# Two experts change places in a routed attention and expert kernel, with SyncE's order of loads and the output buffers

## The chip, the cores and the metric

The kernel runs on one core of a Trainium2 chip. A core has five engines that work side by side: TensorE (matrix products, with a queue of its own for loading weights), VectorE, ScalarE, GpSimd and SyncE, which here issues most of the transfers. The metric is the device time of one execution in microseconds (us).

## The reference

The inputs are q, k, v of 2 batches x 8 heads x 768 tokens x 64, 16 cluster centroids per head, and the weights of the two later stages. What is computed, cut to its core:

```python
# stage 1: attention within clusters
mask   = argmax(q_n @ c_n) == argmax(k_n @ c_n)          # per head
scores = where(mask, q @ k.T / 8, -1e9)
x      = softmax(scores) @ v                             # (2, 768, 512)
# stage 2: one of 8 experts per token
logits, local_gate = x @ w_gate, sigmoid(x @ w_local)
e      = argmax(logits[s]) if s == 0 or local_gate < 0.5 else e_of_the_token_before
x[s]   = softmax(logits[s])[e] * (relu(x[s] @ w1[e]) @ w2[e])   # w1 512x1024, w2 1024x512
# stage 3: gated projection
gate   = sigmoid(causal convolution of x with conv_w, 5 taps)
out    = (gate * (x @ w_val)) @ w_out                    # (2, 768, 512)
```

All of it is wanted in float32. w_val and w_out are given as 64-bit floats and are converted on the chip.

## The kernel before, in words

**Stage 1** runs over 8 groups of two heads. While its last groups run, the routing of tokens is worked out in four quarters of 384 tokens. A quarter's rows (512 values, the softmax weight and the token's number) are scattered by GpSimd into `xslots`, a table in DRAM with a range of rows for each expert, and are also copied whole to `xall` (`keep_rows`), which only the overflow loop reads. Experts 0, 1 and 2 have two ranges, one for each batch.

**Stage 2** takes the experts in 8 places, k = 0 to 7. Places 0, 1, 6 and 7 have fixed experts (the table `AT`, from place to expert); places 2 to 5 take experts 4 to 7 in the order of their token counts, which the chip works out. `CAPS` gives the number of rows (tokens) that a place computes; for the experts with two ranges `ROWS` gives the rows of batch 0 and of batch 1. Tokens beyond these would be done by a loop behind an `If` after the last place. Before the change the widths are 128, 176, 300, 240, 224, 176, 192, 192.

The expert of place 0 is begun early: its batch 0 rows, 128 of them, are loaded, transposed and multiplied during the end of stage 1 (`early_load`, `early_rows`, `early_products`). Place 0 itself then does batch 1. For each place `load_x` reads the rows, `do_x` transposes them on TensorE and casts them to `xhi`, for places 2 to 4 also to a low part `xlo`; `do_mm1` makes the first product (the weights are loaded 128 x 128, the rows stream past as columns), relu on ScalarE and the low part of the result on VectorE; `do_mm2` the second product, in which the rows are loaded as weights and 512 columns of w2 stream past, and `mm2_out` scales and scatters the result to `x2d` in DRAM. Where a tile has 64 rows (`FOLD`, `PACK`) its high and low parts lie side by side in one load of weights, so that it takes 16 matmuls instead of 24; ScalarE and VectorE then add the two halves of the result. Places 6 and 7 do their second product by batch with `do_half`: both places' batch 0 first, then the reload of batch 0 from `x2d`, then both places' batch 1.

**Weights.** An expert has four pieces of 1 MB, (k,0) and (k,1) for the first product, (k,2) and (k,3) for the second. Some are used whole; the others are loaded into one of three staging buffers (`stg`, by `w_stage`), cast by ScalarE (L360, two halves) and reduced to a low part by VectorE (L366, two halves). A staging buffer is free for the next piece when the second subtraction is done. The ring of finished pieces has four places.

**The order.** Nothing is scheduled by a planner: each engine's instructions stand in program order, and SyncE issues its transfers in order too, so that one which waits holds up all behind it. Small steps are spread over the products by `tick`, which is called after each quarter of a first product and after each tile and half of a second one. A tick takes one step from `work` (the casts and subtractions of a piece, the second of them with the load of the next piece), two from `late` (the overflow bookkeeping, on VectorE) and one, sometimes two, from `conv`, the conversion of w_val and w_out. The conversion has 66 steps: 8 chunks, each a load (L260), four VectorE steps (L230 to L238), one of ScalarE (L265, L266), two of GpSimd (L269 and L270, L273) and a store (L276, L277). Its buffer `wspace` is the memory in which the token rows stood before (so its first load waits for `keep_rows(3)`) and into which the rows of stage 3 are reloaded (L1330). What is left of it after batch 0's `do_half` is issued there (L1324).

**Stage 3** transposes the reloaded rows (L1377), makes the value product (L1421, L1422, L1427), the convolution and the gate, and the output product; `project_out` copies a tile of 128 rows from PSUM into a buffer `os` and stores it.

Of the kernel before, what the change touches and what calls it, by code (L numbers as in the profile page):

```python
# [8 lines left out]
F32 = mybir.dt.float32  # L9
# [10 lines left out]
NQT = 6  # L20
NC_ = 16
E = 8
CAPS = (128, 176, 300, 240, 224, 176, 192, 192)
WHOLE = (0, 1, 5, 6, 7)
PACK = 64
AT = {0: 0, 1: 3, E - 2: 2, E - 1: 1}
HALVED = (0, 1, 2)
ROWS = {0: (128, 128), 1: (96, 96), 2: (128, 64)}
V = E + len(HALVED)
NF = len(AT)  # L30
NS = E - NF
SLOT = 428
# [9 lines left out]
def routed_attention_moe_kernel(  # L42
# [289 lines left out]
    def w_stage(at):  # L332
        if pending:
            j = pending.pop(0)
            home[j] = at
            wraw[j] = at.tile([128, 2048], F32, tag="w", name="wraw")
            w_load(j, wraw[j])
# [456 lines left out]

    def early_load():
        EA["xs"] = xin_p.tile([128, 2, S], F32, tag="x", name="exs")[:, 0, :XC]
        nc.sync.dma_start(EA["xs"], xslots[0:128, :])

    def early_rows():
        xs = EA["xs"]  # L800
# [245 lines left out]
    def tick():  # L1046
# [13 lines left out]
    XT, HT, IDS, PW = {}, {}, {}, {}  # L1060
    NT = [-(-c // 128) for c in CAPS]
    FOLD = [
        ROWS[AT[k]][1] == PACK if k and AT.get(k) in HALVED else 0 < (c - 1) % 128 < PACK and n > 1
        for k, (c, n) in enumerate(zip(CAPS, NT))
    ]
    TR = [
# [1 line left out]
    ]  # L1068
    XS = {}

    def load_x(k):
        if k >= E:
            return
        n, rows = NT[k], TR[k]
        XS[k] = xs_p.tile([128, -(-WX[k % 2] // 128), XC], F32, tag=f"xs{k % 2}", name="xs")
        if k == 0:
            nc.sync.dma_start(XS[k][:, 0, :], xslots[E * SLOT:E * SLOT + 128, :])
            return
        if AT.get(k) in HALVED:
            for t, c in enumerate((AT[k], E + HALVED.index(AT[k]))):  # L1080
                nc.sync.dma_start(XS[k][:TR[k][t], t, :], xslots[c * SLOT:c * SLOT + TR[k][t], :])
            return
        if k in AT:
            src = xslots[AT[k] * SLOT:AT[k] * SLOT + CAPS[k], :]
        else:
            src = xslots[bass.ds(turn[k] * SLOT, CAPS[k]), :]
        if FOLD[k] or k == 0:
            for t, r in enumerate(rows):
                nc.sync.dma_start(XS[k][:r, t, :], src[sum(rows[:t]):sum(rows[:t]) + r, :])
        else:  # L1090
            nc.sync.dma_start(XS[k][:rows[0], :n, :], src.rearrange("(t p) c -> p t c", p=rows[0]))
# [140 lines left out]
        for t in sorted(range(n), key=lambda t: (not FOLD[k] or t < n - 1, t)):  # L1232
            mm2_out(k, t)

    def do_half(k, t, *apart):
        YP[k, t] = ps_y.tile([128, 512], F32, tag="y", name="yp")
        for q in range(2):
            mm2_part(k, t, q, *mm2_weights(k, q))
            tick()
        mm2_out(k, t, *apart)  # L1240
# [5 lines left out]
    for n, k in enumerate(free):  # L1246
        turn[k] = nc.sync.value_load(ordi[0:1, n:n + 1], min_val=NF, max_val=E - 1)
    w_stage(stg[2])
    queue_split(R + 2)
    ey = ps_y.tile([128, 512], F32, tag="y", name="ey")  # L1250
    for q in range(2):
# [6 lines left out]
    y = y_p.tile([128, 512], F32, tag="y", name="ysb")  # L1258
    nc.scalar.activation(y, ey, AF.Copy, scale=EA["pw"])
    scatter(x2d, EA["ids"], y, 2 * S, "rows of different tokens")  # L1260
    work += [lambda: None, lambda: None, lambda: keep_rows(3)]
    late += overflow_steps()
    do_mm1(0)
    XS["ready"] = True
    do_mm2(0)
    do_mm1(1)
    for k in range(2, E - 1):
        do_mm1(k)
# [200 lines left out]
    def project_out(b, t, parts=1):  # L1469
        op = OP.pop((b, t))  # L1470
        r0 = S * b + 128 * t
        os_ = fl.tile([128, 512], F32, tag="os", name="os")
        w = 512 // parts
        for n in range(parts):
            cs_ = slice(w * n, w * n + w)
            (nc.vector.tensor_copy if n else nc.scalar.copy)(os_[:, cs_], op[:, cs_])
            (nc.scalar if n else nc.sync).dma_start(out[r0:r0 + 128, cs_], os_[:, cs_])
# [108 lines left out]
```

## Time and profile before

| | |
|---|---|
| median of three runs | 541.88 us (541.17 to 542.16) |
| the profiled execution | 539.74 us, of which its span is 538.1 us |
| TensorE busy | 515.7 us, 96% of the span |
| VectorE, ScalarE, GpSimd busy | 353.1, 310.0, 91.3 us |
| mean granted TensorE clock | 0.99 of full speed |
| moved by all transfers | 108.63 MB, 202 GB/s over the span |

The span reaches from the first to the last instruction; all times in the rows are microseconds from its start. A busy share says how long an engine had an instruction running, not that the time hung on it: for that one looks at the waits. Names such as `wraw<-in_wq_dram` stand for a result and what it is made from, L360 for line 360.

### The profile page before, as it was taken

Reading aid. Unit: us, or ns where it says so; the run is one execution under the profiler, and the core shown is the slowest. Engines: PE = TensorE matmul, PEld = TensorE weight load, DVE = VectorE, ACT = ScalarE, POOL = GpSimd, SP = SyncE. Lnnn points to the kernel's source line nnn. Section 1 sums busy time; section 2 is a strip of 40 time slices with the busy share of each in tenths; the row PEclk is TensorE's granted clock in tenths of the full one; section 3 lists DMA queues with packets and bytes.
Section 4 is the critical chain, followed back from the end, with each engine's and each line's share of the span. In section 5 each row is a group of like instructions: output and inputs, shape, how many; then the busy total and the mean of one; then the engine's idle time right before and its main releaser. Section 6 shows DMA issues by size and latency. Waiting matters only on the chain.

```text
span 538.1 us, 8817 instructions
## 1 busy us (share of the span) xinstructions
PE 515.7 (96%) x3189; PEld 409.4 (76%) x3190; DVE 353.1 (66%) x693; ACT 310.0 (58%) x592; POOL 91.3 (17%) x106
## 2 busy tenths in 40 slices
PE   7898999999999999999999499999999999999996
PEld 3775777777677767776956498979889887899885
DVE  5684767575677877655603679986367673599960
ACT  3696868677776778675112355645334463485632
POOL 5011002020203031000310020523421344100000
PEclk9899999999999999999999889999999999999999
DMA  5876787888887866810665866795978855730023
GB/s 146 225 157 212 154 278 198 242 231 207 267 202 272 191 214 135 294 47 2 201 250 193 314 213 222 242 325 194 362 242 314 311 177 203 266 139 2 19 99 117
DMA packets 35524, 108.63 MB, mean 202 GB/s; under 512 B 4718, under 2 KB 5230, under 8 KB 30869
## 3 DMA queue, kind: packets, MB, share of 16 engines
q1 hardware_dynamic: 32341, 101.15, 60.7%
q0 software_dynamic: 2176, 6.31, 3.2%
q10 hardware_dynamic: 960, 0.58, 0.4%
q8 instruction: 26, 0.43, 0.3%
q14 instruction: 21, 0.17, 0.1%
HBM read 58.39 MB, written 29.83 MB: 164 GB/s over the span
## 4 chain that ended last, share of the span: by engine, by line
PE 41%; DMA 5%; SPq 1%; DVE 1%; ACT 1%; issue 1%; ACTq 0%; DVEq 0%
PE hps L1155 13%; PE yp L1195 4%; PE yp L1197 4%; PE yp L1196 4%; PE vp L1421 2%; PE vp L1427 2%; PE vp L1422 2%; PE op L1467 2%; PE op L1466 2%; PE op L1465 2%; DMA xall<-xnat 2%; PE yp L1192 1%; PE yp L1193 1%; DMA wraw<-in_wq_dram 1%; PE xp L1118 1%
## 5 line engine op out<-in xcount | busy, mean ns | idle before, releaser
L675 DVE TENSOR_REDUCE mx<-s 128x1 f32<-128x768 f32 x96 | 91.6, 954 | 59.5 <-PE s L668 53.4
L704 ACT COPY pt<-tp 128x384 f32<-128x384 f32 x148 | 65.7, 483 | 54.4 <-PE tp L699 54.3
L684 ACT ACTIVATE pexp<-s,mx 128x768 f32<-128x768 f32 x96 | 87.1, 907 | 6.7 <-DVE mx L675 4.5
L699 PE MATMUL tp<-ident,pexp 128*128 128x128 f32 x576 | 81.1, 277 | 0.3 <-DVE pt L702 0.2
L699 PEld LDWEIGHTS tp<-ident,pexp 128*128 128x128 f32 x576 | 68.2, 142 | 7.7 <-ACT pt L704 3.3
L366 DVE TENSOR_TENSOR wlo<-wraw,whi 128x1024 fp32r<-128x1024 f32 x40 | 52.9, 1330 | 29.6 <-ACT whi L360 29.6
L711 PE MATMUL pv<-pt,vt 128*64 128x384 f32 x360 | 67.8, 498 | 0.0
L360 ACT CAST whi<-wraw 128x1024 fp32r<-128x1024 f32 x40 | 40.7, 1046 | 31.8 <-DMA wraw<-in_wq_dram 16.8
L664 PE MATMUL s<-st 128*128 128x384 f32 x188 | 57.3, 386 | 1.5 <-ACT pexp L684 1.5
L1155 PE MATMUL hps<-xhi,wone 128*128 128x192 f32 (+2 forms) x320 | 50.7, 318 | 0.0
L668 PE MATMUL s<-st 80*128 80x384 f32 x188 | 49.0, 342 | 1.4 <-DMA st<-ohr 1.4
L1155 PEld LDWEIGHTS hps<-xhi,wone 128*128 128x128 f32 x320 | 49.0, 195 | 1.6 <-ACT xhi L1124 0.6
L664 PEld LDWEIGHTS s<-st 128*128 128x128 f32 x188 | 28.6, 191 | 17.8 <-issue 7.3
L711 PEld LDWEIGHTS pv<-pt,vt 128*64 128x64 f32 x360 | 21.9, 136 | 23.8 <-issue 23.8
L1162 ACT ACTIVATE h<-hps 128x352 fp32r<-128x352 f32 (+5 forms) x36 | 16.9, 474 | 33.8 <-PE hps L1155 33.7
L1195 PE MATMUL yp<-whi,h 128*112 128x512 f32 (+4 forms) x88 | 35.0, 397 | 0.8 <-ACT h L1162 0.8
L668 PEld LDWEIGHTS s<-st 80*128 80x128 f32 x188 | 34.4, 190 | 1.7 <-issue 1.7
L1197 PE MATMUL yp<-whi,h 128*112 128x512 f32 (+4 forms) x88 | 34.7, 394 | 0.0
L1196 PE MATMUL yp<-wlo,h 128*112 128x512 f32 (+4 forms) x88 | 34.7, 394 | 0.0
L384 POOL TENSOR_TENSOR xx<-xkq,xx 128x768 fp32r<-128x768 f32 x8 | 14.6, 1822 | 117.5 <-ACT xx L378 117.5
L1407 DVE SCALAR_TENSOR_TENSOR gt<-xf,convw_sb,gt 128x768 f32<-128x768 f32 x32 | 32.0, 1015 | 0.4
L1165 DVE SCALAR_TENSOR_TENSOR h<-hps,h 128x128 fp32r<-128x128 f32 (+7 forms) x52 | 18.4, 391 | 16.7 <-ACT h L1162 15.1
(280 smaller groups left out, 893.0 us busy)
## 6 DMA issues: line engine op xcount, KB each, us to landing
wraw<-in_wq_dram SPq DMA_DIRECT2D x20, 1024.0 KB
st<-xx SPq DMA_DIRECT2D x48, 384.0 KB
wone<-in_wq_dram SPq DMA_DIRECT2D x12, 1024.0 KB
xslots<-padrow SPq DMA_DIRECT2D x15, 771.0 KB
xkq<-in_kq_dram SPq DMA_DIRECT2D x15, 384.0 KB
wspace<-in_wd_dram SPq DMA_DIRECT2D x8, 512.0 KB
xall<-xnat SPq DMA_DIRECT2D x4, 771.0 KB
vt<-in_v_dram SPq DMA_DIRECT2D x8, 384.0 KB
```

What stands on the lines that cost most here:

```text
L366: nc.vector.tensor_tensor(lo[:, c], t[:, c], hi[:, c].bitcast(F32), op=ALU.subtract)
L664: nc.tensor.matmul(ps[:, n, :384], st[:, 1, q0:q0 + 128], st[:, 0, 384 * n:384 * n + 384], start=True, stop=False)
L668: nc.tensor.matmul(ps[:, n, :384], st[0:80, 2, q0:q0 + 128], st[0:80, 3, 384 * n:384 * n + 384], start=False, stop=True)
L675: nc.vector.tensor_reduce(mx, ps[:, :, :384], axis=AX.XY, op=ALU.max, negate=True)
L684: nc.scalar.activation(pt, ps[:, :, :384], AF.Exp, bias=mx[:, 0:1], accum_out=Zt[i // 6][:, t, h:h + 1])
L699: nc.tensor.transpose(tp[:, k, :], p[:, 128 * kt:128 * kt + 128], ident)
L704: nc.scalar.copy(dst, tp)
L711: nc.tensor.matmul(PVs[u][64 * h:64 * h + 64, :], Vt[g][:, kt, h, :], PT[u, h][:, kt, :], start=(kt == 0), stop=(kt == NQT - 1), skip_grou ...
L1155: nc.tensor.matmul(hp, a[:, d, fs], c[:, d, :w], start=(n + d == 0), stop=(n + d == len(terms) + 2))
L1195: nc.tensor.matmul(yp[:r], h[:, fa, hi], whv[:, f, :], start=(q == 0 and f == 0), stop=False)
L1196: nc.tensor.matmul(yp[:r], h[:, fa, hi], wlv[:, f, :], start=False, stop=False)
L1197: nc.tensor.matmul(yp[:r], h[:, fa, lo], whv[:, f, :], start=False, stop=(q == 1 and f == 3))
```

## The change

The change has four parts. Place 0 gets expert 1 and place 7 expert 0; the early tile is now expert 1's batch 0, with 128 rows as before, and place 0 computes 72 rows instead of 128. Place 7 has 64 rows of batch 0, which are folded, and 96 of batch 1, with the folded tile put second (`halves`, and the exchange in `do_half`); place 6 has 120 and 64 rows instead of 128 and 64. `keep_rows(3)` is issued by SyncE right behind the load of piece (2,0) instead of by the first tick of place 0's second product; two empty steps stand ahead of the first piece's casts instead of behind them; and the conversion begins after place 0's second product instead of before it. The output tiles have four buffers instead of two.

```diff
-CAPS = (128, 176, 300, 240, 224, 176, 192, 192)
+CAPS = (72, 176, 300, 240, 224, 176, 184, 160)
 WHOLE = (0, 1, 5, 6, 7)
 PACK = 64
-AT = {0: 0, 1: 3, E - 2: 2, E - 1: 1}
+AT = {0: 1, 1: 3, E - 2: 2, E - 1: 0}
 HALVED = (0, 1, 2)
-ROWS = {0: (128, 128), 1: (96, 96), 2: (128, 64)}
+ROWS = {1: (128, 72), 2: (120, 64), 0: (64, 96)}
...
     def early_load():
         EA["xs"] = xin_p.tile([128, 2, S], F32, tag="x", name="exs")[:, 0, :XC]
-        nc.sync.dma_start(EA["xs"], xslots[0:128, :])
+        nc.sync.dma_start(EA["xs"], xslots[AT[0] * SLOT:AT[0] * SLOT + 128, :])
...
     FOLD = [
-        ROWS[AT[k]][1] == PACK if k and AT.get(k) in HALVED else 0 < (c - 1) % 128 < PACK and n > 1
+        PACK in ROWS[AT[k]] if k and AT.get(k) in HALVED else 0 < (c - 1) % 128 < PACK and n > 1
...
+    def halves(k):
+        cols = AT[k], E + HALVED.index(AT[k])
+        return cols[::-1] if ROWS[AT[k]][0] == PACK else cols
+
     def load_x(k):
...
         if k == 0:
-            nc.sync.dma_start(XS[k][:, 0, :], xslots[E * SLOT:E * SLOT + 128, :])
+            c = E + HALVED.index(AT[0])
+            nc.sync.dma_start(XS[k][:CAPS[0], 0, :], xslots[c * SLOT:c * SLOT + CAPS[0], :])
             return
         if AT.get(k) in HALVED:
-            for t, c in enumerate((AT[k], E + HALVED.index(AT[k]))):
+            for t, c in enumerate(halves(k)):
...
-    def do_half(k, t, *apart):
+    def do_half(k, b, *apart):
+        t = b ^ (ROWS[AT[k]][0] == PACK)
         YP[k, t] = ps_y.tile([128, 512], F32, tag="y", name="yp")
...
     w_stage(stg[2])
+    keep_rows(3)
+    work += [lambda: None, lambda: None]
     queue_split(R + 2)
...
-    work += [lambda: None, lambda: None, lambda: keep_rows(3)]
     late += overflow_steps()
     do_mm1(0)
+    do_mm2(0)
     XS["ready"] = True
-    do_mm2(0)
     do_mm1(1)
...
-        os_ = fl.tile([128, 512], F32, tag="os", name="os")
+        os_ = fl.tile([128, 512], F32, tag="os", name="os", bufs=4)
```

## Rows read from the trace of the kernel before

**Rows 1.** The chain of waits, 286 to 309 us: start, duration, what.

```profile
286.72 1.05 ACT whi L360
287.80 1.23 DVE wlo L366
...
292.68 8.17 DMA xall<-xnat
301.00 3.46 DMA wspace<-in_wd_dram
...
305.04 0.69 DVE wspace L231
...
307.80 0.70 DVE xlo L1129
```

**Rows 2.** Timeline of TensorE, 293 to 315 us: start, duration, instruction, [idle before, releaser].

```profile
293.36 4.94 PE L1155 MATMUL hps<-xhi,wone 128*128 128x176 f32 x32
...
308.54 1.45 PE L1118 MATMUL xp<-ident,xs 128*128 128x128 f32 x6 [6.85 <-DVE xlo L1129]
309.92 4.24 PE L1155 MATMUL hps<-xhi,wone 128*128 128x176 f32 x16
313.87 0.83 PE L1155 MATMUL hps<-xhi,whi 128*128 128x300 f32 x4
```

**Rows 3.** Windows: length, busy time by engine (PE first), PEclk, DMA share, GB/s.

```profile
302.00:309.00 7.00, 0.46 (x2) 0.46 (x3) 4.39 (x18) 1.24 (x2) 0.00 (x0) 0.81 0.99 390
```

**Rows 4.** Timeline of TensorE, 440 to 463 us.

```profile
440.08 0.47 PE L1195 MATMUL yp<-whi,h 128*128 128x512 f32 x1 [0.81 <-ACT h L1162]
...
451.30 0.39 PE L1192 MATMUL yp<-whi,h 128*128 128x512 f32 x1
...
460.55 1.47 PE L1377 MATMUL x2p<-ident,x2nat 128*128 128x128 f32 x12
462.98 0.44 PE L1421 MATMUL vp<-xh,whi 128*128 128x384 f32 x1 [0.95 <-ACT xh L1381]
```

**Rows 5.** Timeline of the end of the kernel.

```profile
532.86 0.39 PE L1467 MATMUL op<-whi,gl 128*128 128x512 f32 x1
533.37 1.06 ACT L1476 COPY os<-op 128x512 f32<-128x512 f32 x2 [1.46 <-DMA out_dram<-os]
```

**Rows 6.** Timeline of SyncE's issues: first start, from there to the last one's end.

```profile
279.24 11.41 SPq L326 DMA_DIRECT2D wraw<-in_wq_dram  x2
```

**Rows 7.** Timeline of ScalarE, the first cast of piece (2,1).

```profile
295.71 1.05 ACT L360 CAST whi<-wraw 128x1024 fp32r<-128x1024 f32 x1 [5.81 <-DMA wraw<-in_wq_dram]
```

**Rows 8.** The chain of waits, first products of places 3, 4 and 7.

```profile
337.60 5.39 PE hps L1155 x48
...
364.01 5.36 PE hps L1155 x48
...
428.87 10.41 PE hps L1155 x64
```

**Rows 9.** Timeline of ScalarE in place 7, the conversion's pair and the relu behind it.

```profile
433.77 0.63 ACT L265 ACTIVATE wspace<-wspace 128x512 f32<-128x512 int32 x1
...
434.82 0.49 ACT L1162 ACTIVATE h<-hps 128x384 fp32r<-128x384 f32 x1
```

**Rows 10.** Timeline of GpSimd, 448 to 458 us.

```profile
448.98 1.29 POOL L269 TENSOR_TENSOR wspace<-wspace 128x512 f32<-128x512 f32 x1 [1.06 <-ACT wspace L265]
...
453.04 0.95 POOL L635 DMA_INDIRECT x2d<-ysb,ids  x1 [0.16 <-issue]
...
457.59 0.92 POOL L635 DMA_INDIRECT x2d<-ysb,ids  x1 [3.61 <-DVE ysb L1207]
```

**Rows 11.** SyncE's waits, 450 to 470 us: total, times, longest.

```profile
SPq L1330 <- DMA whd<-wspace: 1.3, 1, 1.3
SPq L1330 <- DMA wld<-wspace: 0.8, 1, 0.8
```

**Rows 12.** Timeline of SyncE, the reload.

```profile
456.04 9.41 SPq L1330 DMA_DIRECT2D x2nat<-x2d  x5
```

## The prediction

> **What bounds the kernel now.** I read the table of busy shares first: TensorE is busy for all but a few per cent of the span, so a gain is either TensorE work that goes away or one of its few waits. The chain of waits, in order of time, shows where those are. The first is at 292 to 309 us: the copy of the last token rows takes 8.17 us, the load of the conversion's first chunk can only start behind it and takes 3.46 us, VectorE stands at the two steps that need this chunk, and place 2's low parts (`xlo`), which TensorE wants, are queued behind them [rows 1]. TensorE's timeline shows the price: 6.85 us idle, and then passes at 265 ns (4.24 us for 16) where the same shape took 154 ns before (4.94 us for 32) [rows 2]; the windows give the reason, a granted clock of 0.81 over 302 to 309 [rows 3], so that it fell to 1.2 GHz some 2.7 us before 309, about 4.6 us into the wait. From there to 440 us the chain is TensorE alone. At 440 it waits 0.81 us for ScalarE. TensorE takes up the reloaded rows at 460.55 without a wait [rows 4]. In the last microseconds the output copies wait for their buffers [rows 5].
>
> **The order at the start.** Removed: the chunk's load no longer waits for the copy, which now goes out right behind piece (2,0). Copy and place 2's rows are 1.4 MB, 3.6 us at the 390 GB/s of a full queue [rows 3]; (2,0), cast from 286.72 in the old run [rows 1], is 0.3 us earlier, so they are through by 290.0, just before SyncE asks for (2,1) at 290.3 (279.24 + 11.41 - 0.34) [rows 6]. That hides them; were the queue slower, (2,1) and all behind it would slip one for one. (2,1) itself isn't earlier: it needs the buffer of (2,0), hence that piece's two casts and two subtractions, and the 0.3 us (56 rows fewer ahead of it, 0.1 MB at that rate) go to the small steps that VectorE now has between the subtractions.
>
> Added: the chunk's load now stands in SyncE's order behind (2,1), (1,2), (1,3) and (3,0). (1,3) waits for the buffer of (2,1), and behind it on SyncE wait (3,0), both first chunks and place 3's rows; VectorE waits for the chunk, TensorE for VectorE. Step by step: (2,1) is there for ScalarE at 295.7, as before [rows 7], 5.4 us after its request. Cast 1.05, subtraction 1.23 [rows 1], small steps some 0.4, second subtraction 1.23: 299.6. (1,3) requested then is in at 305.0 (again 5.4), (3,0) behind it 2.7 us later (1 MB at 390 GB/s), the chunk of 0.5 MB 1.3 us later: 309.0. The two conversion steps are done 1.27 us after a landing and `xlo` takes 0.70 [rows 1]: TensorE goes on at 310.95. It gets there at about 307.2: place 1 starts some 0.4 us earlier than the 293.36 of [rows 2], has 64 passes (9.6 us) and two sets of transposes (1.7 us), an own wait of about 2 us because VectorE only comes free at 299.6, and six passes of place 2 (0.83 us). So a new wait of 3.75 us stands one step later than the old one. In the old run the same six passes end at 313.87 + 0.83 = 314.7. Gain 3.75 us. Bounds: 7.45 us if the chunk is in time (314.7 less 307.2), nothing if it comes 3.75 us later than I say. The chunk's whole chain is made of measured loads, so I take the sum. The rest of the conversion is two ticks later in program order; VectorE then stands to TensorE as it did, and I count nothing for the middle.
>
> **The narrower tiles.** Place 0 goes from 128 to 72 columns, and I count nothing: passes of 240 and of 224 columns both take 112 ns (5.39 and 5.36 us for 48) [rows 8], so loading the weights is a floor there, and 128 columns lie at it (the loads of pieces set the pace behind them anyway). Bounds: nothing to 3 us, the latter if 72 columns ran at their width; the queue would swallow most of it. Place 6 goes from 192 to 184 columns: 163 ns (10.41 us for 64) scaled by width is 156, over 64 passes 0.45 us, on the path. Place 7 goes from 192 to 160, 163 to 136 ns: 1.7 us of TensorE. Only 0.5 arrives: TensorE leaves the branch at 440.08 once ScalarE has done the last relu [rows 4], and the conversion's ScalarE pair, now two ticks later, falls right ahead of that relu. The pair takes 1.05 us (433.77 to 434.82) [rows 9]. The relu of the third quarter is done 7.1 us after the place's start (48 passes at 136 ns, 0.6 for the relu), two casts at 1.0 end at 9.05, the pair at 10.1; the last relu is 0.5 and TensorE goes on 0.3 later, at 10.87 us instead of 11.37 (428.71 to 440.08, the 10.41 us of passes and their wait). The early tile keeps its 128 rows and costs the same.
>
> **The folded tile and the reload.** Batch 0 of place 7 now takes 16 matmuls instead of 24; at 231 ns (451.30 to 460.55 for 40) that is 1.85 us less [rows 4]. But it was the cover of the reload. I count from the end of its last matmul, e, which is 0.15 us after the next tile starts: now 451.45. The scatter follows a folded tile 2.45 us after it (451.30 + 16 x 0.231 + 0.15 = 455.15, to 457.59), where now it follows at 1.6 us (453.04) [rows 10]. Behind it on GpSimd now stand the last chunk's three steps, which in the old order were done before it; they take 3.9 us (448.98 to just before the scatter's 453.04) [rows 10]. SyncE's store of their result waits for them, and the reload writes the same buffer, so it waits for that store: issue 0.3, then waits of 1.3 and 0.8 for the two halves, 2.4 in all [rows 11]. So: 2.45 + 1.05 (the scatter's issue) + 3.9 + 2.4 + 0.2 for the steps between = e + 10.0 for the reload, against e + 4.6 now (456.04) [rows 12]. Its first three row tiles (0.8 MB) need between 2.0 us (the bytes alone) and 4.5 us (456.04 to 460.55, without a wait); I take 4.1, the 2.1 us that the chunk's 3.46 us holds over its bytes, plus 2.0. TensorE is free at e + 9.1, has the last tile at e + 14.1, transposes for 0.9, ScalarE's two casts follow, and the value product starts at e + 16.0; now it starts at e + 11.53 (462.98). That is 4.45 us lost against 1.85 + 0.5 saved: 2.1 us later than before. Bounds: if the three steps were still hidden, a gain of 1.7 us in this stretch (the scatter alone sets the reload); if the reload took its 4.5 us, a loss of 2.5.
>
> **Four output buffers.** The last copies wait for a buffer (1.46 us, then two in a row from 533.37), though the product is done at 533.25 [rows 5]. With four, the last tile's copy starts at about 533.35 instead of 534.05: 0.7 us. No product waits for these buffers, so nothing else moves.
>
> **The sum.** -3.75 - 0.45 + 2.1 - 0.7 = -2.8 us, at full clock in both new waits. A fall of the clock costs between nothing and what it cost before: 16 passes at 4.24 instead of 2.47 us and six transposes at 1.45 [rows 2] where twelve take 1.47 [rows 4], together some 2.3 us. At the start the wait is 3.75 us, shorter than the 4.6 after which it fell, and I take nothing. At the reload TensorE does two short sets of transposes in some 6.9 us, which is nearest to the row of 302 to 309 [rows 3]; much of the slow time would lie in the wait itself, so I take half, 1.2 us. Sum -1.6 us. The profiled execution took 539.74 us and the median of the runs is 541.88, so I carry the difference over: 540.3 us.
>
> The Trainium skill (TensorE: Matmul & The Clock Gate, Part 1) speaks against this: a throttled clock is the default and only recent activity releases it, so each wait should be paid again in slow work behind it. The one long wait of this trace agrees with it. By that rule both new waits would cost the 2.3 us, and the sum would be +1.8.
>
> **The rivals.** *The clock falls in both waits.* -2.8 + 4.6 = +1.8 us, 543.7, slower than before. For it: the old wait of 6.85 us was followed by slow passes. Against it: the new ones are shorter or broken up by work. It decides from 2.8 us of slow work on; from 3.9 us the kernel is measurably slower. *The reload stays hidden*, because GpSimd's steps are faster behind the scatter or SyncE doesn't wait for them: -3.75 - 0.45 - 1.7 - 0.7 = -6.6, 535.3. Against it: GpSimd works in order, and SyncE did wait for these stores [rows 11]. *The chunk is in time at the start*: 3.7 us more than the forecast, -5.3, 536.6. For it: 0.5 MB is a small load; against it: one queue, in order. *The change does not do what it says*: a tile too small for its tokens would start the overflow loop with 4 MB of weights per chunk, 10 us and more at 390 GB/s. The reference's routing gives experts 0, 1 and 2 in the two batches 54 and 88, 88 and 65, 118 and 62 tokens, against 64 and 96, 128 and 72, 120 and 64 rows, so all fit; 1 in 100.
>
> **The numbers.** Forecast 55 in 100 (its own range 538.3 to 542.0); clock in both 19; reload hidden 15; chunk in time 10; overflow 1. Measured runs of this kernel tell about 0.2%, 1.1 us, from no change. Of the forecast's 55, some 36 lie below 540.8 and 18 within 1.1 us of the old time; of the first rival's 19, some 6 are still within. Faster 0.61, same 0.24, slower 0.15. The range 535.0 to 543.4 leaves out the overflow and the outer ends of the rivals.
>
> **What would show it.** In the new trace: the copy issued near 280 us and no SyncE wait for it; VectorE waiting for the chunk until about 309, TensorE waiting for `xlo` there but in front of place 2's low terms; place 0's passes near 112 ns; place 7 at 136 ns and TensorE released by a relu behind the conversion's cast; 16 matmuls in the folded tile, GpSimd's three steps behind its scatter, and a TensorE wait of some 5 us ahead of the value products; no wait of the last copies for buffers; the granted clock in both waits. The prediction is wrong if the middle (314 to 440), in which VectorE has little to spare, gains waits of its own, or if either wait is missing.

## The result, and the profile after

The changed kernel is slower: 544.62 us (median of six runs, 543.46 to 546.24) against 541.62 us (540.42 to 542.16) before, ratio 1.0065 with an interval of 1.0046 to 1.0084. The forecast was 540.3 us with a range that ended at 543.4. The profiled execution of the changed kernel is the longest of the six, 546.24 us with a span of 544.6; the comparisons below go by stretches of the kernel, not by its whole span.

The start, TensorE's timeline (answers to [rows 2]):

```profile
304.08 0.89 PE L1123 MATMUL xp<-ident,xs 128*128 128x128 f32 x6 [2.74 <-DVE xlo L1134]
304.90 4.10 PE L1160 MATMUL hps<-xhi,wone 128*128 128x176 f32 x16
...
312.14 0.54 PE L1160 MATMUL hps<-xlo,whi 128*128 128x300 f32 x2 [2.10 <-DVE xlo L1134]
312.52 1.01 PE L1160 MATMUL hps<-xhi,wlo 128*128 128x300 f32 x4
```

The one wait of 6.85 us has become two, of 2.74 and 2.10 us. Behind both the passes are slow: 16 passes take 4.10 us again, and sets of four take 1.01 us where they take 0.72 a little later. SyncE and VectorE (to [rows 6, 1]; the chunk's load is the first of L260's two):

```profile
279.74 0.37 SPq L326 DMA_DIRECT2D wraw<-in_wq_dram  x1
280.21 0.51 SPq L514 DMA_DIRECT2D xall<-xnat  x1
...
292.40 0.36 SPq L326 DMA_DIRECT2D wraw<-in_wq_dram  x1
292.85 8.44 SPq L324 DMA_DIRECT2D wraw<-in_wq_dram  x2
301.50 0.34 SPq L326 DMA_DIRECT2D wraw<-in_wq_dram  x1
302.08 1.11 SPq L260 DMA_DIRECT2D wspace<-in_wd_dram  x2
```

```profile
310.24 0.43 DVE L230 TENSOR_SCALAR wspace<-wspace 128x512 int32<-128x512 int32 x1 [4.18 <-DMA wspace<-in_wd_dram]
311.31 0.78 DVE L1134 TENSOR_TENSOR xlo<-xp,xhi 128x600 fp32r<-128x600 f32 x1
```

The order is the one foreseen: VectorE stands 4.18 us at the conversion's first step, and place 2's low part is queued behind it. Windows of the start and of the tail (to [rows 3]; PEclk is the third number from the right):

```profile
302.00:309.00 7.00, 4.92 (x23) 4.72 (x24) 3.99 (x18) 1.44 (x2) 0.00 (x0) 0.78 0.89 361
309.00:316.00 7.00, 4.89 (x23) 4.66 (x23) 5.17 (x12) 1.82 (x3) 0.00 (x0) 0.74 0.69 207
459.00:473.00 14.00, 8.14 (x28) 7.37 (x29) 3.90 (x5) 1.76 (x3) 0.00 (x0) 0.52 0.99 359
```

The tail, TensorE's timeline (to [rows 4, 8]):

```profile
427.41 8.86 PE L1160 MATMUL hps<-xhi,wone 128*128 128x160 f32 x64
437.08 0.46 PE L1200 MATMUL yp<-whi,h 128*120 128x512 f32 x1 [0.82 <-ACT wspace L265]
...
461.74 1.09 PE L1384 MATMUL x2p<-ident,x2nat 128*128 128x128 f32 x4 [5.87 <-DMA x2nat<-x2d]
465.27 1.97 PE L1384 MATMUL x2p<-ident,x2nat 128*128 128x128 f32 x8 [2.44 <-DMA x2nat<-x2d]
467.91 0.69 PE L1428 MATMUL vp<-xh,whi 128*128 128x384 f32 x1 [0.68 <-ACT xh L1388]
468.40 0.52 PE L1429 MATMUL vp<-xh,wlo 128*128 128x384 f32 x1
```

Here are three waits where there was one of 0.95 us, and the clock is at 1.2 GHz from 459.5 to 473.1 us: value products start every 0.32 us instead of every 0.17. The chain of waits says what the rows waited for (to [rows 10, 11, 12]):

```profile
450.92 0.92 POOL x2d L635
...
451.84 1.32 POOL wspace L269
453.16 1.25 POOL wspace L270
...
454.49 1.63 POOL wspace L273
...
456.14 2.31 DMA wld<-wspace
...
458.59 0.32 SPq L1337
...
458.96 6.26 DMA x2nat<-x2d
```

The scatter of place 7's folded tile, GpSimd's three conversion steps, the store of their result and the reload follow one another without a gap, as the prediction had them. At the end (to [rows 5]) five copies follow one another without waiting for a buffer:

```profile
535.22 3.31 ACT L1483 COPY os<-op 128x512 f32<-128x512 f32 x5 [6.51 <-issue]
```

I cut each profiled span into stretches that can be compared. A runs from SyncE's request of piece (2,0) to place 6's second product (before: 279.24 to 440.08), B from there to the first value product (462.98), C from there to the end of the span. Times and ratios are those of the runs; the kernel before had medians from 540.5 to 541.6 beside them.

| kernel | A | B | C | median | ratio to before, interval |
|---|---|---|---|---|---|
| before | 160.8 | 22.9 | 75.1 | 541.62 | |
| after | 157.3 | 30.8 | 76.7 | 544.62 | 1.0065 (1.0046 to 1.0084) |
| e1 conversion begun earlier | 158.0 | 29.7 | 75.7 | 543.95 | 1.0056 (1.0038 to 1.0074) |
| e2 two steps in the halves | 157.2 | 28.4 | 74.2 | 543.09 | 1.0041 (1.0026 to 1.0056) |
| e3 order alone | 158.1 | 27.4 | 77.9 | 544.14 | 1.0071 (1.0045 to 1.0097) |
| e4 tiles alone | 159.9 | 25.2 | 76.5 | 543.40 | 1.0044 (1.0019 to 1.0069) |
| f1 four buffers alone | 160.9 | 23.3 | 74.3 | 539.70 | 0.9988 (0.9968 to 1.0008) |
| f2 products in the wait | 157.6 | 28.8 | 74.2 | 541.08 | 1.0021 (0.9993 to 1.0049) |
| f3 no copy | 155.7 | 29.3 | 75.9 | 544.37 | 1.0077 (1.0051 to 1.0102) |
| f4 conversion done early | 156.9 | 23.1 | 74.2 | 534.49 | 0.9896 (0.9860 to 0.9933) |
| g1 and later at the start | 153.8 | 21.3 | 74.2 | 531.33 | 0.9833 (0.9788 to 0.9877) |
| g2 old kernel, conversion early | 162.2 | 22.9 | 74.2 | 539.54 | 0.9972 (0.9956 to 0.9988) |
| g3 as g1, products at the start | 153.9 | 21.0 | 74.3 | 531.11 | 0.9807 (0.9771 to 0.9843) |
| g4 tiles, conversion early | 159.4 | 21.0 | 74.2 | 537.81 | 0.9935 (0.9910 to 0.9960) |
| h1 last steps held back | 157.8 | 27.3 | 76.4 | 542.06 | 1.0031 (1.0010 to 1.0052) |
| h2 without the branch | 155.1 | 31.0 | 75.7 | 543.87 | 1.0059 (1.0032 to 1.0085) |

From before to after, A gained 3.5 us, B lost 7.9 and C lost 1.6. Two executions of one order differ by up to 2 us in A or B (B of the changed kernel, f2 and f3), so a row of this table carries no more than that. The profiled execution of e2 is the fastest of its runs (540.56 us) and that of g2 the slowest (541.75).

### The profile page after: what moved, and what is told of

Same layout as the page of the kernel before. It is cut to its first block, busy times and chain, and to the rows that moved or that the text cites. A ratio compares the mean times of both kernels' runs of the same rounds, so it can differ in the third digit from the quotient of the medians.

```text
span 544.6 us, 8798 instructions
## 1 busy us (share of the span) xinstructions
PE 517.2 (95%) x3181; PEld 409.8 (75%) x3182; DVE 356.5 (65%) x700; ACT 309.2 (57%) x593; POOL 96.4 (18%) x106
## 4 chain that ended last, share of the span: by engine, by line
PE 78%; DMA 11%; DVE 3%; SPq 2%; issue 2%; ACT 2%; POOL 1%; POOLq 0%; DVEq 0%; ACTq 0%
PE pv L711 12%; PE tp L699 11%; PE hps L1160 11%; PE s L664 7%; PE s L668 6%; PE yp L1201 3%; PE yp L1200 3%; PE yp L1202 3%; DMA wraw<-in_wq_dram 2%; PE vp L1428 2%; DMA x2d<-ysb,ids 2%; PE po L736 2%; PE vp L1429 2%; PE vp L1434 2%; PE op L1473 2%; PE op L1472 2%
## 5 line engine op out<-in xcount | busy, mean ns | idle before, releaser
L366 DVE TENSOR_TENSOR wlo<-wraw,whi 128x1024 fp32r<-128x1024 f32 x40 | 55.8, 1406 | 25.5 <-ACT whi L360 25.3
L1160 PE MATMUL hps<-xhi,wone 128*128 128x176 f32 (+3 forms) x320 | 48.4, 311 | 0.0
L1160 PEld LDWEIGHTS hps<-xhi,wone 128*128 128x128 f32 x320 | 46.7, 194 | 1.6 <-issue 0.5
L1167 ACT ACTIVATE h<-hps 128x352 fp32r<-128x352 f32 (+6 forms) x36 | 16.2, 453 | 38.7 <-PE hps L1160 38.6
L1200 PE MATMUL yp<-whi,h 128*112 128x512 f32 (+4 forms) x80 | 31.8, 397 | 0.8 <-ACT wspace L265 0.8
L1201 PE MATMUL yp<-wlo,h 128*112 128x512 f32 (+4 forms) x80 | 31.5, 394 | 0.0
L1202 PE MATMUL yp<-whi,h 128*112 128x512 f32 (+4 forms) x80 | 31.5, 394 | 0.0
L635 POOL DMA_INDIRECT xslots<-xnat,idx x12 | 12.0, 1002 | 93.3 <-DVE red L626 69.7
```

The source lines that it names most:

```text
L366: nc.vector.tensor_tensor(lo[:, c], t[:, c], hi[:, c].bitcast(F32), op=ALU.subtract)
L1160: nc.tensor.matmul(hp, a[:, d, fs], c[:, d, :w], start=(n + d == 0), stop=(n + d == len(terms) + 2))
L1200: nc.tensor.matmul(yp[:r], h[:, fa, hi], whv[:, f, :], start=(q == 0 and f == 0), stop=False)
L1201: nc.tensor.matmul(yp[:r], h[:, fa, hi], wlv[:, f, :], start=False, stop=False)
L1202: nc.tensor.matmul(yp[:r], h[:, fa, lo], whv[:, f, :], start=False, stop=(q == 1 and f == 3))
```

## The experiments

**e1 to e4: one suspect at a time.** The first four each undid one thing that could hold the reload, or did one part of the change alone.

e1, the conversion begins before place 0's second product again:

```diff
-    do_mm2(0)
     XS["ready"] = True
+    do_mm2(0)
```

> The changed kernel, but the conversion begins before place 0's second product, as in the old kernel; the copy of the last rows stays early. Reload theory (the loss comes from the last chunk's GpSimd steps standing behind the folded tile's scatter, which delays the reload by some 8 us and drops the clock there): with two ticks more the steps lie before the scatter, TensorE's wait ahead of the value products falls from 9 us (5.87 + 2.44 + 0.68) to 1 to 3 us; and the chunk's load is asked for two pieces earlier, so the 2.10 us wait in place 2 goes too: 534 to 538 us. Start theory (the new order of loads at the start and the slow clock there eat the gain, the reload's wait matters little): the reload's part stays as it is, 540 to 543 us.

Measured 543.95 us, missing both. At the start one wait of 6.07 us took the place of the two. GpSimd's last steps now ended at 451.34, before the scatter, but SyncE issued the stores only at 455.77: it stood 6.4 us at the branch of the overflow loop (what held it there is not shown), and the reload came at 459.51. Taking the steps out of the scatter's way uncovered the next thing behind them.

e2, one conversion step more after each half of a `do_half`:

```diff
             tick()
+            if conv:
+                conv.pop(0)()
         mm2_out(k, t, *apart)
```

> The changed kernel, with a second step of the conversion behind each tick of batch 0's halves of places 6 and 7, so that all of it is issued ahead of the last scatter; nothing else differs, the start is that of the changed kernel. Reload theory: the scatter is as late as before (ScalarE still waits for VectorE's steps), but the three GpSimd steps overlap that wait; the reload starts some 3 to 4 us earlier, the slow clock behind it goes: 536 to 541 us, at least 3.5 below the changed kernel. Start theory: no change, 543.5 to 545.5 us.

Measured 543.09, again missing both, if narrowly on one side. The steps are now in front of the scatter (451.84), but that is later itself, 15.6 us after place 6's second product starts instead of 13.8, and so the reload came only 0.2 us earlier (21.3 instead of 21.5). Most of the 2.4 us by which B is shorter lies behind the reload, where the rows came sooner, in an execution 2.5 us faster than the median of e2.

e3, the old tiles and two buffers with the new order (the edit is to the kernel before):

```diff
     w_stage(stg[2])
+    keep_rows(3)
+    work += [lambda: None, lambda: None]
     queue_split(R + 2)
...
-    work += [lambda: None, lambda: None, lambda: keep_rows(3)]
...
-    XS["ready"] = True
     do_mm2(0)
+    XS["ready"] = True
```

> The old kernel with only the new order: early copy, empty steps first, conversion after place 0's second product. Tiles and output buffers are the old ones. Reload theory: a gain of 1.5 to 3 us at the start, and at the reload the three GpSimd steps stand behind the scatter also of the unfolded tile, which costs 4 to 7 us with the clock: 543 to 548 us. Theory that the fold alone exposes the reload: the unfolded tile's 24 matmuls still cover it, only the gain of the start remains: 538.5 to 540.5 us.

e4, the new tiles with the old order and two buffers: e3's edit undone in the changed kernel, and `bufs=4` away.

> The old kernel with only the new places and tiles (72, 184, 160 rows, the folded tile); order and output buffers are the old ones. Reload theory: place 7 is 1.7 us shorter, place 6 0.4, the folded tile 1.85; the conversion is done before the scatter, which follows the fold 0.9 us later, so the reload costs 1 to 3 us back: 538 to 541 us. Theory that the fold alone exposes the reload: a wait of 5 us and more ahead of the value products and the slow clock behind it, 542 to 545 us.

Both are slower than the kernel before, by 0.7% and 0.4%. In e3 B is 27.4 us although the cover is the old one: the order alone takes the reload out from under it. In e4 B is 25.2 although the conversion is as early as before: the new tiles do so too. Place 7 is 1.7 us shorter and the folded tile 1.85, which no run took apart. The time of e3 lies where the reload theory had it. That of e4 misses it (538 to 541) and lies in the other theory's range, but its waits ahead of the value products are 1.82 and 1.35 us and not the 5 that this one asked for. Each alone costs more in B than it gains in A. The old order and the old tiles fitted each other with nothing to spare.

**f1: four buffers alone.**

```diff
-        os_ = fl.tile([128, 512], F32, tag="os", name="os")
+        os_ = fl.tile([128, 512], F32, tag="os", name="os", bufs=4)
```

> The old kernel with four output buffers and nothing else. If the buffers are worth what the copies at the end waited for, 0.7 us: 540.8 against 541.5, ratio 0.9987, and the ScalarE copies of the last two tiles start without a wait for a transfer. Rival: a buffer that is free earlier only moves the wait to the store behind it, and the time stays as it is, ratio 1.000.

The median is 0.8 us lower and C shrinks by 0.8; the interval of the ratio still holds 1. C is 74.2 to 74.3 in every kernel that has four buffers and a full clock, which is what carries this term.

**f2: products in the wait for the rows.**

```diff
-    for t in range(3):
+    keep_warm(wide_ps(0, "spin2")[:, 0, :], 27)
+    x2_tiles(0, 0, 1, nc.vector.tensor_copy)
+    keep_warm(wide_ps(0, "spin3")[:, 0, :], 9)
+    for t in range(1, 3):
         x2_tiles(0, t, 1, nc.vector.tensor_copy)
```

> The changed kernel with 27 products of 512 bfloat16 columns (some 5.8 us) put into TensorE's wait for the reloaded rows and 9 (1.9 us) between the first and the second rows; their result is read by nobody. Theory that the clock's fall behind this wait is a part of the loss of its own: granted clock full from 455 us to the end, value products at 0.16 instead of 0.32 us, some 3 us faster than the changed kernel: 541.6, ratio 1.000 to the old kernel. Rival (the clock is no loss of its own, since the rows and ScalarE's casts set the pace until about 474 us anyway): within 0.5 us of the changed kernel, 544.6, ratio 1.006.

Measured 541.08, 3.5 us below the changed kernel (2.4 by the ratios). TensorE's timeline of f2:

```profile
454.85 6.00 PE L117 MATMUL spin<-onesb 128*128 128x512 bf16 x27
460.68 0.60 PE L1384 MATMUL x2p<-ident,x2nat 128*128 128x128 f32 x4
461.12 2.11 PE L117 MATMUL spin<-onesb 128*128 128x512 bf16 x9
463.19 1.09 PE L1384 MATMUL x2p<-ident,x2nat 128*128 128x128 f32 x8
465.01 0.45 PE L1428 MATMUL vp<-xh,whi 128*128 128x384 f32 x1 [0.73 <-ACT xh L1388]
465.29 0.34 PE L1429 MATMUL vp<-xh,wlo 128*128 128x384 f32 x1
```

The granted clock is 1.00 over 455 to 473, B is still long (28.8), and C is back at 74.2. So the clock's fall behind the reload's wait is a loss of its own, 2.5 us in C, and the wait before it is the rest.

**f3: no copy** (the last quarter's rows are not copied to `xall`).

```diff
-    keep_rows(3)
     work += [lambda: None, lambda: None]
```

> The changed kernel without the copy of the last quarter's rows (only the overflow loop, which does not run, would read them; this is the part left out). Theory that the copy, now right behind piece (2,0) on the queue, makes that piece late: (2,0) lands 1.2 us earlier, some 7.4 us after its request, all pieces and the conversion's first chunk behind it too, TensorE's second wait for xlo is 0.9 instead of 2.1 us, place 1's second product starts 1.2 us earlier: 543.4 against 544.6, ratio 1.004. Rival (the copy hides behind the pieces, as the prediction had it; the piece is slow for another reason): start and time as in the changed kernel, ratio 1.006.

The time does not answer: 544.37 us, as the changed kernel. The trace says a little: (2,0) is cast 8.46 us after its request, against 8.8 to 10.7 in the ten traces that have the new order with the copy and 7.5 to 8.5 in the five with the old order. If the copy delays the piece, it is by about 1 us, and TensorE still waited 2.29 us for `xlo`. It is no main cause.

**f4: the conversion is done early**, two steps in each tick from place 5's first product on.

```diff
-            if conv and beats[0] % 4 == 3:
+            if conv and (hurry or beats[0] % 4 == 3):
                 conv.pop(0)()
...
     for k in range(2, E - 1):
+        if k == 5:
+            hurry.append(1)
         do_mm1(k)
```

> The changed kernel with two conversion steps in each tick from place 5's first product on, so that the conversion is over before place 7's product ends. Theory that what is left of the conversion stands in the reload's way (GpSimd's steps behind the scatter, SyncE's stores, ScalarE's pair ahead of ysb, VectorE's slowed subtractions): the reload is asked for 0.3 us behind the scatter's landing, at about 450.5 instead of 458.6, TensorE's wait for the rows is under 1 us, the clock stays full, and the time is 8 us less than the changed kernel's: 536.5, ratio 0.991. Rival A (the scatter itself and the rows' landing set the reload, the conversion only fills the time): reload at 455 or later, 542 or more. Rival B: VectorE, with two steps in each tick, becomes late for place 5's and 6's products, new waits between 380 and 430 us eat the gain: 540 to 542.

Measured 534.49 us, ratio 0.9896 to the kernel before where 0.991 was expected, and 10 us below the changed kernel (9 by the ratios). TensorE's timeline:

```profile
455.32 0.63 PE L1386 MATMUL x2p<-ident,x2nat 128*128 128x128 f32 x4 [0.65 <-DMA x2nat<-x2d]
457.15 1.09 PE L1386 MATMUL x2p<-ident,x2nat 128*128 128x128 f32 x8 [1.21 <-DMA x2nat<-x2d]
458.97 0.44 PE L1430 MATMUL vp<-xh,whi 128*128 128x384 f32 x1 [0.73 <-ACT xh L1390]
```

Waits of 5.87 and 2.44 us have become 0.65 and 1.21, and the clock stays full. No wait came up in the middle (100.33 us from place 1's second product to place 7, 100.35 in the changed kernel), so VectorE had room for the steps. The reload itself still came 4.7 us behind the scatter's issue (447.84 to 452.56), not the 0.3 us behind its landing that I had expected from a landing at 450.2; SyncE had only come through the branch at 451.9.

**g1: and begun later at the start.** As f4, but the conversion begins after place 1's first product and the two steps in each tick with place 4. The edit is to f4.

```diff
-    XS["ready"] = True
     do_mm1(1)
+    XS["ready"] = True
     for k in range(2, E - 1):
-        if k == 5:
+        if k == 4:
             hurry.append(1)
```

> As f4 (two conversion steps in each tick), but the conversion begins after place 1's first product and the two steps in each tick begin with place 4. Theory that TensorE's second wait at the start (1.24 us in f4, 2.10 in the changed kernel) is VectorE standing 4.1 us at the conversion's first step until its chunk lands at 310.4, with the low part of place 2 queued behind: VectorE makes this low part at about 307, the second wait is gone, the first (3.6 us, for piece (2,1)) stays, place 1's second product starts 1.2 to 2 us earlier, 533.0 against 534.5, ratio 0.987. Rival: VectorE is over 90% busy from 320 to 360 us, so the steps that are moved there make place 2's and 3's low parts late, with TensorE waits of their own in that stretch: no gain or a loss, 534.5 or more.

531.33 us, ratio 0.9833 where 0.987 was expected: 10 us below the kernel before. VectorE in g1:

```profile
302.50 0.76 DVE L1134 TENSOR_TENSOR xlo<-xp,xhi 128x600 fp32r<-128x600 f32 x1
...
303.68 1.21 DVE L366 TENSOR_TENSOR wlo<-wraw,whi 128x1024 fp32r<-128x1024 f32 x1
...
305.21 0.78 DVE L1134 TENSOR_TENSOR xlo<-xp,xhi 128x600 fp32r<-128x600 f32 x1
```

The second low part is made at 305.21 instead of 311.31, TensorE's second wait is gone, and A is 3.5 us shorter than in the changed kernel, 3.1 shorter than in f4. What I had taken as given in the start's sum, that the chunk must come before the low part, was only a place in VectorE's order.

**g2: the old kernel with the conversion done early and four buffers; g4: the new tiles and four buffers with the old order, conversion done early.** The edit is f4's.

> The old kernel with four output buffers and with two conversion steps in each tick from place 5 on; tiles and order are the old ones. Theory that the early conversion is worth something only together with a shorter cover (in the old kernel TensorE took up the rows without a wait): 0.7 us from the buffers and at most 0.8 from the wait at the last relu, 539.5 against 540.5, ratio 0.998. Rival: the early conversion is a gain of its own, whatever the tiles, and f4 owes its 6 us to it: 536 or less, ratio 0.991.

> The changed kernel's tiles and four output buffers with the old order at the start, and two conversion steps in each tick from place 5 on. By the prediction's terms with the reload out of the way the tiles bring 0.45 + 1.7 + 1.85 us and the buffers 0.7, so 535.8 against 540.5, ratio 0.991, and the new order's worth is the difference to f4, 1.3 us (place 1's second product started 1.1 to 1.7 us earlier in the changed kernel). Rival: the order is worth nothing or less, since the old one begins the conversion earlier: 534.5 or less, as f4 or better.

g2 comes to 0.9972, as the first theory had it: an early conversion is worth nothing while the cover is long enough. g4 comes to 0.9935, below the kernel before but slower than f4 (0.9896), so with the tail mended the tiles are worth about 0.4% beyond g2. The new order would be worth another 0.4%, but here the intervals of g4 and f4 overlap, and in the stretches f4 gains 2.5 us in A and loses 2.1 in B: its worth is not shown. The forecast of 535.8 us for g4 was 2 us too low.

**g3: as g1, with 14 products ahead of the transposes for which TensorE waits at the start.**

```diff
+                if k == 1 and (q, fp) == (1, 0):
+                    keep_warm(ps_h.tile([128, 512], F32, tag="h", name="spin4"), 14)
                 if k < E - 1 and (q, fp) in ((0, 1), (1, 0)):
```

> As g1, with 14 products of 512 bfloat16 columns (3.0 us, read by nobody) ahead of the transposes for which TensorE waits at the start. Theory that the half clock behind that wait is paid in full once no second wait follows: 22 passes and transposes at full clock, 1.8 to 2.4 us faster than g1, 531, ratio 0.983. Rival: VectorE or the next piece is late by as much anyway, so the time is g1's within 0.5 us.

The trace shows the effect: the clock is full over 299 to 314 (0.89 in g1), and 16 passes take 2.65 us where they take 4.33 in g1. The medians, 531.11 and 531.33 us, don't show it. In the profiled execution piece (2,0) was cast 1.7 us later after its request than in g1, which may have taken up the gain there. Inconclusive.

**h1: f4 with only GpSimd's last three steps and their store held back to where the changed kernel has them; h2: the changed kernel without the overflow loop and its branch.** The edit of h1 is to f4.

```diff
-        if conv and XS.get("ready"):
+        if len(conv) > (4 if hurry else 0) and XS.get("ready"):
...
-            if conv and (hurry or beats[0] % 4 == 3):
+            if len(conv) > (4 if hurry else 0) and (hurry or beats[0] % 4 == 3):
```

> As f4, but the last chunk's three GpSimd steps and its store are held back until batch 0's second products are issued, where the changed kernel has them; the chunk's VectorE and ScalarE steps are done early, as in f4. Theory of the prediction (GpSimd's steps behind the scatter and the store that waits for them): the reload comes 3.9 us for the steps and 2.4 us for the store behind the scatter's issue, 19.5 us after place 6's second product starts (f4 16.7, the changed kernel 21.5), the value products 3 us later than in f4, with a fall of the clock: 539 to 540, ratio 0.997. Rival (the VectorE and ScalarE steps of the conversion, ahead of the folded tile's result, are what holds the reload; GpSimd's steps cost little once these are away): within 1.5 us of f4, 534.5 to 536, ratio 0.990.

542.06 us, ratio 1.0031: the three steps and the store alone cost 1.4% against f4, of the 1.7% by which the changed kernel is slower than f4, and 2 us more than the theory expected. The chain of waits of h1:

```profile
448.48 0.93 POOL x2d L635
449.42 1.33 POOL wspace L269
450.75 1.24 POOL wspace L270
...
452.06 1.64 POOL wspace L273
...
453.72 2.34 DMA wld<-wspace
...
456.21 0.32 SPq L1339
...
456.58 4.57 DMA x2nat<-x2d
```

The reload is issued 19.7 us after place 6's second product starts (456.21 less 436.53); 19.5 was expected. It takes 7.7 us from the scatter to the reload, as in the changed kernel (450.92 to 458.59). So in the profiled executions the prediction's own mechanism makes 4.2 of the 7.7 us by which the changed kernel's B is longer than f4's, and 2.1 of the 2.5 in C. Of the other 3.5 us in B, 1.9 lie in front of the scatter, which the changed kernel issues 13.8 us after place 6's second product starts and h1 11.95, and 1.7 between the reload's issue and the value products (9.3 us against 7.6).

For h2 (what is left out is the loop for overflowing tokens, which these inputs don't have):

```diff
-    nch = nc.values_load(infoi[0:1, 0:1], min_val=0, max_val=NCH)
-    with tc.If(nch > 0, preferred_fallthrough_block=False):
...
     do_half(E - 2, 0)
```

> The changed kernel without the If and the overflow loop in it (which doesn't run on these inputs; this is the part left out). Theory that the branch delays the tail: VectorE (0.9 us) and SyncE (6 us at the branch) go on at once, the last chunk's VectorE steps start some 1 to 2 us earlier, the stores and the reload too: value products 28 to 29 us after place 6's second product starts instead of 30.8, 542.5, ratio 1.002. Rival: the engines are held by the conversion's own chain, not by the branch; as the changed kernel, ratio 1.006.

543.87 us: the tail is as long as with the branch (B 31.0), so the branch is not the cause. But it showed what a wait that I had read wrongly is. TensorE's timeline of h2:

```profile
426.61 8.86 PE L1160 MATMUL hps<-xhi,wone 128*128 128x160 f32 x64
435.19 0.50 PE L1200 MATMUL yp<-whi,h 128*120 128x512 f32 x1
```

Without the branch TensorE goes from place 7's first product to place 6's second without a wait.

## Why the prediction was wrong

**The folded tile and the reload: right chain, wrong sizes; this is the step that failed.** The prediction put the reload at e + 10.0 us, the last row tile at e + 14.1 and the value products at e + 16.0, and with that the whole stretch at 2.1 us, its clock at 1.2. Here e is 446.5 us (437.08 plus 40 matmuls at 0.231, plus 0.15), the reload is at e + 12.1, its second set of rows is used at e + 18.8, the value products start at e + 21.4. These terms make up the 5.4 us, with 0.1 for issues:

- 2.0 us: the scatter came at e + 4.4 instead of e + 2.45. I let ScalarE turn to the folded result as soon as it was there. But the conversion's ScalarE pair stands ahead of it and waited 3.94 us for VectorE's last step; VectorE was late because its two subtractions of the last piece took 3.87 us, with GpSimd's steps beside them, instead of the 2.36 of the later pair in the old trace, and because the last chunk's seven steps all came behind them. Where the pair is done early the scatter comes at e + 2.6 (f4 and h1: 447.84 and 448.48, with e at 445.3 and 445.9), as I had it. From the scatter to the reload I was right: 7.6 us forecast, 7.7 measured.
- 2.6 us: I took 4.1 us from the reload to its last tile, from the old trace in which batch 1's rows are asked for 9 us later. Here it is 6.7, of which 6.26 stand in the chain after the issue. All five requests go out within 3.3 us here and within 9.5 in f4, which has 4.16, so one might think that the first three share the queue with the others. The runs don't bear that out: e1 and e2 ask for all five within 2.9 and 3.2 us and have 4.39 and 4.09. With the changed kernel's tail f3 has 4.74 and h2 5.57. Why it is 6.26 in this execution stays open.
- 0.7 us: transposes and casts at half clock, 2.64 us instead of 1.9.

The rows behind the first term, from the timelines of VectorE, GpSimd and ScalarE in the changed kernel:

```profile
438.80 3.87 DVE L366 TENSOR_TENSOR wlo<-wraw,whi 128x1024 fp32r<-128x1024 f32 x2
...
439.31 2.27 POOL L270 TENSOR_TENSOR wspace<-wspace 128x512 f32<-128x512 f32 x1
...
447.52 0.63 ACT L265 ACTIVATE wspace<-wspace 128x512 f32<-128x512 int32 x1 [3.94 <-DVE wspace L237]
```

The later pair of subtractions in the kernel before:

```profile
443.64 2.36 DVE L366 TENSOR_TENSOR wlo<-wraw,whi 128x1024 fp32r<-128x1024 f32 x2
```

Those behind the second, SyncE's requests in the changed kernel and, in e2, the requests and the chain of waits behind them:

```profile
458.59 3.29 SPq L1337 DMA_DIRECT2D x2nat<-x2d  x5
```

```profile
457.52 3.16 SPq L1339 DMA_DIRECT2D x2nat<-x2d  x5
...
457.89 4.09 DMA x2nat<-x2d
```

From place 7's start to the value products the loss is 6.2 us (467.91 - 427.41 against 462.98 - 428.71) where the sum had 2.1, and the clock takes 2.5 more behind it (f2) where it had 1.2. These two terms alone turn -1.6 into +3.8, and the start, below, adds 2.2. In the profiled executions the difference comes to 6.5 us, in the medians to 3.0; B of f2 and f3, where the tail is the same but for f2's products in the wait, is 28.8 and 29.3 us (31.0 in h2), so the profiled execution shows this loss near its upper end.

**The start: half as much.** Forecast -3.75 us; place 1's second product starts 47.3 us after the request of (2,0) instead of 48.9 (327.06 and 328.14), a gain of 1.6. The chain of loads was good to 1 us: TensorE was to go on at 310.95 and does at 312.14, in an execution that asked for (2,0) 0.5 us later. There the gain is still 3.2 us (32.4 us after the request; the old run was at the same pass 35.6 after it). Missing is the clock. I held that waits shorter than the old one leave it alone; it fell behind waits of 2.74 and of 2.10 us. The 16 slow passes behind the first cost nothing, since TensorE had to wait for `xlo` once more; those behind the second do, and from there to place 1's second product it takes 14.9 us instead of 13.3. The 0.83 us that I took for six passes is a row of four, which is an error of some 0.1 us.

**Place 7: 1.7 us instead of 0.5**, because the wait in front of place 6's second product is not the last relu. TensorE goes on at 437.08, before that relu (437.39) has begun; the wait is 0.82 us as before, and without the branch it is gone (h2). The profile's releaser there is whatever ended last.

**Place 0 and place 6.** 32 passes of 72 columns take 3.69 us, so the floor held. Place 6 was to give 0.45 us; the middle, from place 1's second product to place 7, is 100.35 us instead of 100.57.

**The output buffers: right**, 0.7 us forecast, 0.8 in C and in f1's median.

**The rivals.** The rival with the clock falling in both waits came nearest (543.7 us), and half of its reason was right: the clock did fall in both. Its -1.45 us for the start (-3.75 + 2.3) is near what came (-1.6); it had the reload's time as the forecast did. The price of a fall, 2.3 us, is 2.5 by the rows that the prediction names (1.77 for the passes, 0.7 for the transposes), and 2.5 is what f2 gives back in C. The rule of the Trainium skill that the prediction cited for it (TensorE: Matmul & The Clock Gate, Part 1: the throttle is the default, activity releases it) agrees with both stretches here, 0.78 and 0.74 at the start and 0.52 at the tail. The prediction gave it 19 in 100 on the strength of a single old wait. The rival on the other side of the forecast, the reload hidden, is what f4 makes true: -6.6 us forecast, -6.0 measured.

## What to carry to other kernels

When cover is taken away from a transfer, list everything that stands ahead of it on every engine, not only the longest chain: here the end of the conversion was out of sight only as long as the cover was long, and removing one obstacle (e1, e2) brought up the next. Work that only has to be done at some time is best finished well before the point where the cover ends; that edit alone turned the change from 0.65% slower into 1.0% faster, and with the first chunk out of place 2's way 1.7% (g1). A wait's price is the wait and the slow clock behind it, and several short waits need not be cheaper than a long one: A is 157.3 us with waits of 2.74 and 2.10, and 158.0 with one of 6.07 (e1).

## What the runs showed of the hardware

- The granted clock fell to 1.2 GHz behind waits of 2.7 and 2.1 us with some 6 us of work between them (0.78 and 0.74 over the two stretches), and at the tail it stayed there until 473 us, while TensorE did two short sets of transposes and 16 products in the 17.5 us after its halves ended. Products that nobody reads kept it at 2.4 GHz (1.00 over 455 to 473 us in f2 and over 299 to 314 in g3).
- GpSimd's steps on 128 x 512 floats took 2.29, 2.27 and 2.15 us beside VectorE's subtractions, and 1.32, 1.32 and 1.62 where VectorE did little; the two subtractions took 3.87 us beside them and 2.36 without (a pair of which only the last 1.1 us lay beside them took 2.35). The Trainium skill (GPSIMD Engine Reference, 1. Specifications) says that GpSimd shares its interfaces to the on-chip memory with VectorE, with contention when VectorE has two inputs there; these subtractions have two, and the trace agrees.
- At a branch that is not taken TensorE stood 0.82 us (437.08, and none in h2) and SyncE up to 6.4 us (e1). What SyncE waited for is not shown, and without the branch the tail was no shorter (h2).
